# Retention attention and two feed-forward blocks on one core: two half units of a head pair in one TensorE visit, q by transposes, no filling matmuls in eight visits

## The chip, the cores and the metric

The kernel runs on one core of one Trainium2 chip. The metric is the device time of the core in microseconds, taken as the median of several executions. One further execution is recorded by the hardware profiler; all rows below come from that record of the kernel before.

## The reference

Three stages follow each other. The first is attention with a decay and without a softmax, the second a feed-forward block that takes the maximum of three projections, the third a gated feed-forward block.

```python
# attention: B, H, S, D = 4, 8, 576, 64
scores = scale * np.matmul(q, k.transpose(0, 1, 3, 2))
gamma = 1.0 - 2.0 ** (-5.0 - np.arange(H))
rel = pos[:, None] - pos[None, :]
Dmat = np.where(rel >= 0, gamma[:, None, None] ** rel, 0.0)
x = np.matmul(scores * Dmat, v)          # then (B*S, H*D) = (2304, 512)

# first block: w1, w2, w3 are (512, 768), w_out is (768, 512)
h = np.maximum(np.maximum(x @ w1, x @ w2), x @ w3)
x = h @ w_out

# second block: w_gate, w_val are (512, 1536), w_out2 is (1536, 512)
g = x @ w_gate
out = (g / (1 + np.exp(-g)) * (x @ w_val)) @ w_out2
```

## The kernel before

**Attention in units.** A unit is half of the 576 tokens (288, three chunks of 96) of one pair of heads of one batch; there are 32, in the order batch, head pair, half. Within a chunk the scores are computed directly; what earlier chunks contribute goes through a 64x64 state per head, which is carried from chunk to chunk with a decay. So a unit needs k and q with the head dimension on the partitions (kt and qg; qg is q times the decay g), k and v with the tokens on the partitions, and the states.

**What a unit does.** `a_prep(n)` makes ks (GpSimd), kt and qg. For the first PT = 12 units k and q come in rows of tokens and TensorE turns them: k by three transposes with the identity (L225), q by six matmuls against a diagonal matrix `dia` that holds the decay (L228); ScalarE copies both out of PSUM (L230). From unit 12 on k and q are loaded a second way by `t_load` (L188, eight loads of 32 columns, that is 128-byte pieces, for a pair of units, into a tile qk of which there are two); VectorE turns them in blocks of 32x32 and multiplies q by `cst_g`. `a_score(n)` is the group of six matmuls s (L248) and a multiplication by the decay mask on VectorE, giving pT. `a_state(n)` is the group m_ps (L264; four or six matmuls) and the chain of states on VectorE. `a_value(n)` is the group o_ps of states by q (L285; four or six) and of v by pT (L289; six). ScalarE then takes the upper part xh out of o_ps and VectorE the rest xl.

**Slices.** The first feed-forward block works on 288 tokens and 128 of the 768 columns at a time: one slice is twelve matmuls of 128x288 (L358) on the two-part splits of x and of the weights; ScalarE (w1) or VectorE (w2, w3: a maximum) takes it out of PSUM into hmax, and every third slice is stored. PSUM has two buffers for slices, one tile each for s, m_ps, o_ps and tp.

**Weights.** w1, w2 and w3 come as 18 tiles of 512 KB of double words, here w0 to w17 in the order of use (L106). Each is turned into two tiles by six steps: two passes on ScalarE (L115, L121), two instructions and a sum on VectorE (L123, L124, L126), wh on ScalarE (L134) and wlo on GpSimd (L136). A tile is loaded when the third step before it in the same buffers has been reached (`win_load(i + 4)`). After them come the weights of the second block (`early_steps`), some steps in each visit from unit 16 on.

**Order.** The order of all engines is the order of the program text. `visit(n)` does the value matmuls of unit n, the loads that are due, the states and scores of unit n + 1, and then a number of slices with `a_prep(n + 2)` and the conversion steps between them. Units 0 to 7 have no slices: their visits are the attention alone, and after each stands one filling matmul on zeros (`spin`, L380). Visits 8 to 13 have four slices, 14 and 15 six, later ones five. SyncE issues nearly all loads and stores, in program order, and a load into a buffer that is still read holds back those behind it. `a_load` of a pair is done in the odd visits, `t_load` in the even ones, for the pair two further on; `cst_g` is loaded in visit 9.

## Time and profile before

| | |
|---|---|
| median of three executions | 833.75 us (833.35 to 836.33) |
| the profiled execution | 833.75 us, span 831.6 us |
| TensorE busy | 817.6 us, 98% of the span |
| VectorE, ScalarE, GpSimd busy | 68%, 38%, 25% of the span |
| time in L358 (the slices' matmuls), three lines of 576 | 173.1 + 169.7 + 169.6 us |
| granted clock of TensorE | 1.00 in all stages |

The attention with its slices takes the first third of the span: the value matmuls of unit 11 begin at 67.92 us and those of the last unit at 273.3 us. Matmuls are pipelined, so the durations of neighbouring ones overlap and what one costs is read from start to start. In the timeline an f32 matmul of the attention counts twice, so "x12" is six matmuls. The DMA share is the mean over 16 engines, and a value near 1 says that they had work all the time.

### The profile page before, as it was taken

What the parts mean: (1) busy time and instruction counts of PE and PEld (TensorE: products, weight loads), DVE (VectorE), ACT (ScalarE), POOL (GpSimd) and SP (SyncE); (2) the same over time, 40 slices, a digit from 0 to 9 for tenths busy, and PEclk for the clock granted to TensorE, in tenths of its full rate; (3) what the DMA queues carried; (4) which work ended last, traced back from release to release, by engine and by line L of the source; (5) the groups of instructions that cost most, each with busy time, mean ns of one, the idle gap of its engine ahead of it and who ended that gap; (6) DMA issues with size and microseconds to landing.
All of it is one profiled execution on the core that took longest, in us unless ns stands there. A gap on an engine that the chain in (4) does not pass through costs nothing.

```text
span 831.6 us, 15514 instructions
## 1 busy us (share of the span) xinstructions
PE 817.6 (98%) x5933; PEld 762.7 (92%) x5933; DVE 563.4 (68%) x1007; ACT 315.0 (38%) x633; POOL 208.7 (25%) x194
## 2 busy tenths in 40 slices
PE   9999999999999999999999999999999999999998
PEld 6799899998989999999988999999998999999996
DVE  2678857787874354476587888888899455555554
ACT  3554523333321233565445553444443222332220
POOL 4243320000000002342023333233332333222331
PEclk9999999999999999999999999999999999999999
DMA  9999849999981223865555444334420716565522
GB/s 177 230 202 235 174 119 243 254 251 239 253 225 61 81 99 99 247 180 157 198 207 191 146 159 165 143 137 165 161 80 13 266 49 243 216 226 213 204 92 76
DMA packets 165801, 142.94 MB, mean 172 GB/s; under 512 B 101344, under 2 KB 137952, under 8 KB 165728
## 3 DMA queue, kind: packets, MB, share of 16 engines
q1 hardware_dynamic: 164368, 141.56, 57.7%
q8 instruction: 46, 0.75, 0.4%
q10 hardware_dynamic: 1360, 0.41, 0.2%
q14 instruction: 27, 0.22, 0.1%
HBM read 93.70 MB, written 48.23 MB: 171 GB/s over the span
## 4 chain that ended last, share of the span: by engine, by line
PE 68%; issue 14%; DVE 7%; POOL 6%; ACT 2%; DMA 1%; SPq 1%; POOLq 0%; ACTq 0%; DVEq 0%
PE ps L358 26%; PE g L786 17%; PE ps L763 11%; PE ps L715 6%; POOL gl L834 3%; PE s L248 2%; PE o_ps L289 2%; POOL p L807 2%; PE o_ps L285 2%; PE m_ps L264 1%; SPq L188 1%; PE tp L228 1%; PE psz L380 1%; DMA w<-in_moe_w_val_dram 1%; DVE wz L124 0%
## 5 line engine op out<-in xcount | busy, mean ns | idle before, releaser
L358 PE MATMUL ps<-xl,wh 128*128 128x288 f32 x576 | 173.1, 300 | 3.7 <-DVE hmax L364 3.1
L358 PE MATMUL ps<-xh,wh 128*128 128x288 f32 x576 | 169.7, 295 | 0.0
L358 PE MATMUL ps<-xh,wlo 128*128 128x288 f32 x576 | 169.6, 294 | 0.0
L834 POOL TENSOR_TENSOR gl<-p,gh 128x384 fp32r<-128x384 f32 x72 | 85.8, 1209 | 293.7 <-ACT gh L833 293.7
L763 PE MATMUL ps<-wp,gh 128*128 128x512 f32 (+1 forms) x436 | 135.3, 391 | 0.4 <-DVE acc L768 0.3
L358 PEld LDWEIGHTS ps<-xl,wh 128*128 128x128 f32 x576 | 108.0, 188 | 7.6 <-DVE hmax L364 4.0
L358 PEld LDWEIGHTS ps<-xh,wh 128*128 128x128 f32 x576 | 108.1, 188 | 0.0
L358 PEld LDWEIGHTS ps<-xh,wlo 128*128 128x128 f32 x576 | 108.1, 188 | 0.0
L763 PEld LDWEIGHTS ps<-wp,gh 128*128 128x128 f32 x436 | 80.7, 188 | 14.4 <-DVE acc L768 1.0
L364 DVE TENSOR_TENSOR hmax<-ps,hmax 128x288 f32<-128x288 f32 x96 | 43.6, 455 | 68.6 <-PE ps L358 61.9
L763 PE MATMUL ps<-wp,gl 128*128 128x512 f32 (+1 forms) x218 | 85.6, 393 | 0.0
L768 DVE TENSOR_TENSOR acc<-ps,acc 128x512 f32<-128x512 f32 (+1 forms) x91 | 62.2, 684 | 33.6 <-PE ps L763 31.6
L786 PE MATMUL g<-xhB,wa 128*128 128x384 f32 x288 | 73.4, 336 | 0.0
L786 PE MATMUL g<-xhT,wc 128*128 128x384 f32 x288 | 73.2, 335 | 0.0
L546 POOL TENSOR_TENSOR hl<-hf,hh 128x384 fp32r<-128x384 f32 x26 | 30.0, 1163 | 129.3 <-DMA h_d<-hmax 77.4
L833 ACT ACTIVATE gh<-p 128x384 fp32r<-128x384 f32 x72 | 37.8, 525 | 60.4 <-DVE p L837 53.2
L822 ACT ACTIVATE sb<-u 128x384 f32<-128x384 f32 x36 | 18.9, 525 | 110.0 <-DVE u L820 110.0
L218 POOL TENSOR_TENSOR ks<-kn,cst_a 96x384 f32<-96x384 f32 (+1 forms) x32 | 26.3, 825 | 126.1 <-PE m_ps L264 107.6
L786 PEld LDWEIGHTS g<-xhB,wa 128*128 128x128 f32 x288 | 52.1, 188 | 0.0
L786 PEld LDWEIGHTS g<-xhT,wc 128*128 128x128 f32 x288 | 52.0, 188 | 0.0
L814 DVE TENSOR_TENSOR p<-g,p 128x384 f32<-128x384 f32 x36 | 19.9, 554 | 46.4 <-PE g L786 40.6
L362 ACT ACTIVATE hmax<-ps 128x288 f32<-128x288 f32 x48 | 19.7, 410 | 81.4 <-PE ps L358 81.2
(119 smaller groups left out, 1710.9 us busy)
## 6 DMA issues: line engine op xcount, KB each, us to landing
w<-in_moe_w_out_dram SPq DMA_DIRECT2D x18, 512.0 KB, 4.1
w<-l_d SPq DMA_DIRECT2D x28, 256.0 KB, 2.9
h_d<-hmax SPq DMA_DIRECT2D x48, 144.0 KB, 3.3
w<-in_moe_w_dram SPq DMA_DIRECT2D x12, 512.0 KB, 5.9
w<-in_moe_w_gate_dram SPq DMA_DIRECT2D x12, 512.0 KB, 5.8
w<-in_moe_w_val_dram SPq DMA_DIRECT2D x12, 512.0 KB, 6.0
vn<-in_v_dram SPq DMA_DIRECT2D x16, 288.0 KB, 7.6
out_dram<-acc SPq DMA_DIRECT2D x17, 256.0 KB, 2.0
```

The source lines that it names most:

```text
L218: pool.tensor_tensor(u["ks"][:, 0:nk], u["k"][:, 0:nk], sc, ALU.mult)
L358: pe.matmul(ps, l[:, ksl], r, start=n == 0, stop=n == 3 * KD - 1)
L362: act.activation(mx[hb], ps, ACTF.Copy)
L364: dve.tensor_tensor(mx[hb], ps, mx[hb], ALU.max)
L546: (dve if fi in (3, 5) and hx else pool).tensor_tensor(hl, hf, f(hh), ALU.subtract)
L715: pe.matmul(ps[:, 0:HT], l[:, es], rr, start=n == 0, stop=n == 3 * F1 - 1)
L763: pe.matmul(ps[:, cs], l[:, sl], r[:, cs], start=n == 0, stop=n == 3 * GRP - 1)
L768: dve.tensor_tensor(a[:, cs], ps[:, cs], a[:, cs], ALU.add)
L786: pe.matmul(ps, l[:, ks], r[:, kc], start=first and n == 0, stop=n == 5, skip_group_check=True)
L814: dve.tensor_tensor(p5, g2, p5, ALU.add)
L833: act.activation(gh[half], t, ACTF.Copy)
L834: pool.tensor_tensor(gl[half], t, f(gh[half]), ALU.subtract)
```

## The change

- **Pairs.** From unit 12 on the two halves of a head pair are one visit (`visit_pair`, ten of them, for pairs 6 to 15): one group of ten and one of twelve matmuls for the values (`pair_value`), one group of ten for the states and one of twelve for the scores of the next pair (`pair_next`), then as many slices as the two visits had: eight, twelve, and ten from pair 8 on. States and chain follow in `late` steps between the slices. PSUM is given out anew in visit 11 (`swap_banks`, after xl of unit 11): four banks for scores and states, two for values.
- **q by transposes.** Units 0 to 11 transpose q as they do k. The tables `dia` go; ScalarE copies kt alone and VectorE multiplies q by `cst_g` on its way out of PSUM. `cst_g` is loaded at the start on ScalarE's queue, behind its loads of q.
- **Filling matmuls.** The eight behind visits 0 to 7 go. Those ahead of the first visit stay.
- **Loads.** `t_load` is done in each of visits 8 to 11 (pairs 6 to 9) and in each pair visit (for the pair three further on). So the qk tile of pair 9 is loaded in visit 11 and again in the visit of pair 6. `kq` has four buffers, not three.
- **Conversions.** In the visits of pairs 6 and 7 the plan has five and four tiles, spread over the first eight slices; from pair 8 on there are 17 early steps a pair, where two visits had 18.

```diff
+    def swap_banks():
+        nonlocal psa_cm, psa
+        psa_cm.__exit__(None, None, None)
+        psa_cm = tc.tile_pool(name="ps_pair", bufs=1, space=PSUM)
+        psa = psa_cm.__enter__()
...
-        kq = att.tile([P, 2, C], F32, name="kq", tag="kq", bufs=3)
+        kq = att.tile([P, 2, C], F32, name="kq", tag="kq", bufs=4)
...
             tp = psa.tile([P, 2, 512], F32, name="tp", tag="tp")
-            for c in range(NC):
-                pe.transpose(tp[:, 0, c * CK:(c + 1) * CK], u["k"][:, c].rearrange("p h d -> p (h d)"), ident)
-            for c in range(NC):
-                for e in range(2):
-                    pe.matmul(tp[64 * e:64 * e + 64, 1, c * CK:(c + 1) * CK], u["q"][:, c, e],
-                              dia[pr][:, e], start=True, stop=True)
-            act.activation(kq, tp[:, :, 0:C], ACTF.Copy)
+            for i, nm in enumerate("kq"):
+                for c in range(NC):
+                    pe.transpose(tp[:, i, c * CK:(c + 1) * CK], u[nm][:, c].rearrange("p h d -> p (h d)"), ident)
+            act.activation(kt, tp[:, 0, 0:C], ACTF.Copy)
+            dve.tensor_tensor(qg, tp[:, 1, 0:C].rearrange("p (c m) -> p c m", c=NC), g, ALU.mult)
...
+    def pair_value(j):
+        o = psa.tile([P, 2, 512], F32, name="o_ps", tag="o2")
...
+        for xh, xl, h in low:
+            dve.tensor_tensor(xl, o[:, h, 0:C], f(xh), ALU.subtract)
+
+    def pair_next(j):
...
+        s = psa.tile([P, 4, 512], F32, name="s", tag="s4")
+        m = [s[:, h, C + c * D:C + (c + 1) * D] for h in range(2) for c in range(NC - h)]
...
+        return [chain_states, lambda: weigh(0), lambda: weigh(1)]
...
         if n % 2:
             a_load(n // 2 + 3)
-        else:
-            t_load(n // 2 + 2)
+        if n >= PT - 4:
+            t_load(n - 2)
...
-        a_state(n + 1)
+        if n + 1 < PT:
+            a_state(n + 1)
         low()
-        a_score(n + 1)
+        if n + 1 < PT:
+            a_score(n + 1)
+            late = []
+        else:
+            swap_banks()
+            late = pair_next(PT // 2)
+        ahead = [n + 2] if n < PT - 2 else [PT, PT + 1] if n < PT - 1 else [PT + 2, PT + 3]
...
+    def visit_pair(j, slices, convs):
+
+        share = sharing(min(slices, 8 if convs else slices), convs, j >= 8)
+        pair_value(j)
+        share(0)
+        a_load(j + 3)
+        t_load(j + 3)
...
+        late = pair_next(j + 1)
+        for x in range(slices + 1):
+            if late:
+                late.pop(0)()
+            if x in (3, 5):
+                a_prep(2 * j + 4 + (x == 5))
+            if x:
+                share(x)
+            if x < slices:
                 f_some(1)
...
     a_load(0, "q", 2, act)
+    act.dma_start(out=cst_g, in_=consts[:, O_G:NCONST])
     a_load(0, "v")
...
-    for n in range(NU):
+    for n in range(PT):
...
-        if n == 9:
-            sp.dma_start(out=cst_g, in_=consts[:, O_G:NCONST])
-        visit(n, *((0, 0) if n < 5 else (0, 1) if n < 8 else (4, 2) if n < 13 else (4, 3) if n < 14 else (6, 2) if n < 16 else (5, 0)))
-        if n < 8:
-            spin(1)
-        if n == 15:
+        visit(n, *((0, 0) if n < 5 else (0, 1) if n < 8 else (4, 2)))
+    for j in range(PT // 2, NU // 2):
+        visit_pair(j, *((8, 5) if j == 6 else (12, 4) if j == 7 else (10, 0)))
+        if j == 7:
             ask(1)
```

The order on the engines changes at three places. The first is TensorE around the visits of units 1 and 2, which have no slices: `tp` are the transposes of the unit two further on, `psz` the filling matmul. Before:

```order
L225 MATMUL tp<-cst_a,kn 128x96 x3
L228 MATMUL tp<-dia_83,qn 64x96 x6
L380 LDWEIGHTS zero
L380 MATMUL psz<-zero 128x512
L285 MATMUL o_ps<-kq,st 64x96 x6
L289 MATMUL o_ps<-pT,vn 64x96 x6
L264 MATMUL m_ps<-vn,ks 64x64 x6
L248 MATMUL s<-kq 96x96 x6
```

And after:

```order
L228 MATMUL tp<-cst_a,kn 128x96 x3
L228 MATMUL tp<-cst_a,qn 128x96 x3
L285 MATMUL o_ps<-kq,st 64x96 x6
L289 MATMUL o_ps<-pT,vn 64x96 x6
L264 MATMUL m_ps<-vn,ks 64x64 x6
L248 MATMUL s<-kq 96x96 x6
```

The value matmuls of a unit now stand right behind the transposes of the unit after the next, with three transposes of q where six matmuls stood.

The second place is TensorE at the start of a pair. Before, the second unit of the pair has its own four groups, with slices (L358) ahead and behind:

```order
L358 MATMUL ps<-xh,wh 128x288
L285 MATMUL o_ps<-kq,st 64x96 x6
L289 MATMUL o_ps<-pT,vn 64x96 x6
L264 MATMUL m_ps<-vn,ks 64x64 x6
L248 MATMUL s<-kq 96x96 x6
L358 MATMUL ps<-xl,wh 128x288
```

After, one visit has the groups of both units (and the slices are at L417):

```order
L417 MATMUL ps<-xh,wh 128x288
L304 MATMUL o_ps<-kq,st 64x96 x10
L309 MATMUL o_ps<-pT,vn 64x96 x12
L332 MATMUL s<-vn,ks 64x64 x10
L339 MATMUL s<-kq 96x96 x12
L417 MATMUL ps<-xl,wh 128x288
```

Four groups instead of eight, the states now in the tile of the scores, and one change from and to the slices instead of two.

The third place is SyncE's queue from visit 8 on, behind the qk set of pair 6. `w64e` and `w_` are weight tiles, `kn` and `vn` a pair's rows of k and v, `qk` its eight transposed loads, `h_d` stores of hmax. Before, the first two rows are w7 and w8, the third weight tile w9, the next w10 and w11:

```order
L106 DMA w_774<-in_moe_w_dram 128x4x128
L106 DMA w64e<-in_moe_w_dram 128x4x128
L504 DMA cst_g<-in_consts_dram 128x384
L167 DMA kn<-in_k_dram 96x12x64
L167 DMA vn<-in_v_dram 96x12x64
L106 DMA w64e<-in_moe_w_dram 128x4x128
L345 DMA h_d_57<-hmax 128x288
L345 DMA h_d_58<-hmax 128x288
L106 DMA w_986<-in_moe_w_dram 128x4x128
L188 DMA qk<-in_k_dram 32x18x32 x4
L188 DMA qk<-in_q_dram 32x18x32 x4
L106 DMA w_1053<-in_moe_w_dram 128x4x128
```

And after, from w8 on:

```order
L108 DMA w64e<-in_moe_w_dram 128x4x128
L169 DMA kn<-in_k_dram 96x12x64
L169 DMA vn<-in_v_dram 96x12x64
L190 DMA qk<-in_k_dram 32x18x32 x4
L190 DMA qk<-in_q_dram 32x18x32 x4
L108 DMA w64e<-in_moe_w_dram 128x4x128
L404 DMA h_d_57<-hmax 128x288
L404 DMA h_d_58<-hmax 128x288
L108 DMA w_947<-in_moe_w_dram 128x4x128
L190 DMA qk<-in_k_dram 32x18x32 x4
L190 DMA qk<-in_q_dram 32x18x32 x4
L108 DMA w_1014<-in_moe_w_dram 128x4x128
```

The set of pair 7 has moved ahead of w9, that of pair 8 stands ahead of w11, and `cst_g` has gone from the queue. Further on the set of pair 9 comes twice, ahead of w13 and ahead of w15:

```order
L190 DMA qk<-in_k_dram 32x18x32 x4
L190 DMA qk<-in_q_dram 32x18x32 x4
L404 DMA h_d_58<-hmax 128x288
L108 DMA w64e<-in_moe_w_dram 128x4x128 x2
L169 DMA kn<-in_k_dram 96x12x64
L169 DMA vn<-in_v_dram 96x12x64
L190 DMA qk<-in_k_dram 32x18x32 x4
L190 DMA qk<-in_q_dram 32x18x32 x4
L108 DMA w_1352<-in_moe_w_dram 128x4x128
```

## Rows read from the trace of the kernel before

**Rows 1.** Table by stretches: us, PE, PEld, DVE, ACT, POOL busy, PEclk, DMA share, GB/s.

```profile
0.00:40.00 40.00, 37.61 (x553) 27.52 (x553) 17.79 (x41) 17.28 (x35) 14.32 (x25) 1.00 1.13 199
40.00:100.00 60.00, 59.95 (x643) 56.28 (x640) 47.08 (x99) 31.57 (x63) 24.09 (x20) 1.00 0.96 213
...
120.00:240.00 120.00, 118.43 (x1203) 112.55 (x1202) 90.83 (x193) 43.44 (x89) 10.32 (x12) 1.00 0.97 249
```

**Rows 2.** Timeline of ScalarE (start, us, engine, line, operation, idle before): w4, w15.

```profile
44.09 0.68 ACT L115 ACTIVATE wz<-w64e 128x512 f32<-128x512 f32 x1 [1.14 <-DMA w64e<-in_moe_w_dram]
44.67 0.40 ACT L362 ACTIVATE hmax<-ps 128x288 f32<-128x288 f32 x1
...
91.21 0.66 ACT L115 ACTIVATE wz<-w 128x512 f32<-128x512 f32 x1
```

**Rows 3.** Tile views of w9, w10, pair 7's last q, w15: issue (first, last), landing.

```profile
L106 SPq DMA_DIRECT2D w64e<-in_moe_w_dram x1: 2948/2948/2948, 56.8 to 56.8; - x1
DMA to landing us min/median/max: 7.3/7.3/7.3
...
L106 SPq DMA_DIRECT2D w<-in_moe_w_dram x1: 423/423/423, 61.0 to 61.0; - x1
DMA to landing us min/median/max: 5.7/5.7/5.7
...
L188 SPq DMA_DIRECT2D qk<-in_q_dram x2: 498/917/1336, 67.0 to 68.4; - x2
DMA to landing us min/median/max: 2.8/2.9/3.0
...
L106 SPq DMA_DIRECT2D w<-in_moe_w_dram x1: 433/433/433, 84.5 to 84.5; - x1
DMA to landing us min/median/max: 4.4/4.4/4.4
```

**Rows 4.** Waits of TensorE from 20 to 118 us: total, times, longest.

```profile
PE ps L358 <- DVE hmax L364: 1.2, 1, 1.2
```

**Rows 5.** Timeline of TensorE, visits of units 1 and 2.

```profile
13.24 0.71 PE L285 MATMUL o_ps<-kq,st 64*64 64x96 f32 x12
13.88 0.72 PE L289 MATMUL o_ps<-pT,vn 96*64 96x96 f32 x12
14.43 0.52 PE L264 MATMUL m_ps<-vn,ks 96*64 96x64 f32 x12
14.88 0.75 PE L248 MATMUL s<-kq 64*96 64x96 f32 x12
15.56 0.47 PE L225 MATMUL tp<-cst_a,kn 96*128 96x96 f32 x3
15.96 0.72 PE L228 MATMUL tp<-dia,qn 96*64 96x96 f32 x12
16.61 0.39 PE L380 MATMUL psz<-zero 128*128 128x512 bf16 x1
16.93 0.55 PE L285 MATMUL o_ps<-kq,st 64*64 64x96 f32 x8
17.40 0.72 PE L289 MATMUL o_ps<-pT,vn 96*64 96x96 f32 x12
17.95 0.40 PE L264 MATMUL m_ps<-vn,ks 96*64 96x64 f32 x8
18.28 0.75 PE L248 MATMUL s<-kq 64*96 64x96 f32 x12
```

**Rows 6.** Timeline of TensorE: third slice of unit 8; value matmuls of unit 11.

```profile
45.99 0.40 PE L358 MATMUL ps<-xl,wh 128*128 128x288 f32 x1
46.23 0.30 PE L358 MATMUL ps<-xh,wlo 128*128 128x288 f32 x1
46.36 0.29 PE L358 MATMUL ps<-xh,wh 128*128 128x288 f32 x1
...
67.92 0.47 PE L285 MATMUL o_ps<-kq,st 64*64 64x96 f32 x6
```

More of the change, by code (lines that the diff above doesn't have):

```diff
@@ L42 @@
 O_E = O_KS + NP * 2
-O_Q = O_E + NP
-O_S = O_Q + H
+O_S = O_E + NP
 O_M = O_S + H
@@ L96, in retention_moe @@
     g_t = cst_g.rearrange("p (r m) -> p r m", r=NP)
-    dia = [att.tile([CK, 2, CK], F32, name=f"dia{i}", tag=f"dia{i}", bufs=1) for i in range(NP)]
     d_t = [att.tile([CK, 2, CK], F32, name=f"dm{i}", tag=f"dm{i}", bufs=1) for i in range(NP)]
@@ L294, in a_value @@
         return lambda: dve.tensor_tensor(xl, o, f(xh), ALU.subtract)
+    def pair_value(j):
+        o = psa.tile([P, 2, 512], F32, name="o_ps", tag="o2")
+        us = [U.pop(2 * j + h) for h in range(2)]
+        for h, u in enumerate(us):
+            for c in range(1 - h, NC):
+                for e in range(2):
+                    hd = slice(64 * e, 64 * e + 64)
+                    pe.matmul(o[hd, h, c * CK:(c + 1) * CK], u["st"][hd, h * NC + c], u["qg"][hd, c],
+                              start=c == 1 - h, stop=False, skip_group_check=True)
+        for h, u in enumerate(us):
+            for c in range(NC):
+                for e in range(2):
+                    pe.matmul(o[64 * e:64 * e + 64, h, c * CK:(c + 1) * CK], u["v"][:, c, e], u["pT"][:, e, c],
+                              start=False, stop=True, skip_group_check=True)
+        b, _, pr = units[2 * j]
+        low = []
+        for h in range(2):
+            xh, xl = [ffn.tile([P, C], F32R, name=f"x{x}", tag=f"x{x}{pr}", bufs=4) for x in "hl"]
+            act.activation(xh, o[:, h, 0:C], ACTF.Copy)
+            xs[(2 * b + h, pr)] = (xh, xl)
+            low.append((xh, xl, h))
+        for xh, xl, h in low:
+            dve.tensor_tensor(xl, o[:, h, 0:C], f(xh), ALU.subtract)
@@ L380, in spin, with sharing @@
             pe.matmul(ps, zero[:, 0:P], zero, start=True, stop=True)
-    def visit(n, slices, convs):
+    def sharing(spread, convs, joins):
         plan = list(conv_plan(convs))
@@ L387, in share @@
             nonlocal done
-            upto = len(plan) * (j + 1) // (slices + 1)
+            upto = len(plan) * (j + 1) // (spread + 1)
             for step in plan[done:upto]:
@@ L392, in share, with visit @@
             done = upto
-            if n >= 16:
+            if joins:
                 for _ in range(1 if j % 2 else 2):
                     next(early, None)
+        return share
+    def visit(n, slices, convs):
+        share = sharing(slices, convs, False)
         low = a_value(n)
@@ L414, in visit @@
             if j < slices:
+                f_some(1)
+    def visit_pair(j, slices, convs):
[4 more added lines that the diff above has]
+        t_load(j + 3)
+        if j % NP == NP - 1:
+            fq.extend((2 * (j // NP) + h, *w) for w in win_units for h in range(2))
+        late = pair_next(j + 1)
+        for x in range(slices + 1):
+            if late:
+                late.pop(0)()
+            if x in (3, 5):
[3 more added lines that the diff above has]
+            if x < slices:
                 f_some(1)
@@ L475, in retention_moe @@
     a_load(0, "q", 2, act)
+    act.dma_start(out=cst_g, in_=consts[:, O_G:NCONST])
     a_load(0, "v")
     def tables(pr):
-        for t, sc, src in ((dia, q_t, ident), (d_t, s_t, mask)):
-            pool.tensor_tensor(t[pr], src.unsqueeze(1).to_broadcast([CK, 2, CK]),
-                               sc[:, 2 * pr:2 * pr + 2].unsqueeze(2).to_broadcast([CK, 2, CK]), ALU.mult)
+        pool.tensor_tensor(d_t[pr], mask.unsqueeze(1).to_broadcast([CK, 2, CK]),
+                           s_t[:, 2 * pr:2 * pr + 2].unsqueeze(2).to_broadcast([CK, 2, CK]), ALU.mult)
     tables(0)
```

34 lines of the change are left out of this document (30 added, 4 removed).

## The prediction

> **What bounds the kernel now.** I read the table by stages first [rows 1]. TensorE is busy in 59.95 of the 60 us from 40 to 100 and in 118.43 of the 120 from 120 to 240, at a granted clock of 1.00, so what leaves TensorE could leave the total. The same rows say that a second resource is full: the DMA share is 1.13 up to 40 us, 0.96 up to 100, 0.97 from 120 to 240. So I then read the loads, each by its time to landing, against the instruction that needs it. They land in the order of their issue. ScalarE has waited 1.14 us for weight tile w4 when it starts its first pass at 44.09 [rows 2], and the loads behind it take 4.4 to 7.3 us from issue to landing [rows 3]: w9 lands at 56.8 + 7.3 = 64.1, w15 at 84.5 + 4.4 = 88.9, 2.3 ahead of its first pass at 91.21 [rows 2, 3]. The trace of before therefore balances TensorE against a full stream of loads whose lead over ScalarE is some 0 to 2 us. TensorE's own waits are small: 1.2 us for hmax between 20 and 118 [rows 4].
>
> **The change part by part.** *Filling matmuls and q.* One filling matmul takes 0.32 us from its start to the next (16.61 to 16.93); eight are 2.6 us. The q matmuls of a unit take 0.65 (15.96 to 16.61) [rows 5]; three more transposes cost 0.40 if they are as those of k (15.56 to 15.96) [rows 5], less if the two groups run on without a step between; I take 0.35, so 0.30 a unit and 3.6 us for twelve. TensorE's work before the slices of unit 8 (ten units' transposes and eight filling matmuls) falls by some 5.6 us.
>
> *The multiply by g goes to VectorE.* Twelve instructions over 288 columns of PSUM; the nearest row is ScalarE's hmax of that shape, 0.40 [rows 2]. VectorE has 22 us free of the first 40 [rows 1], so they hide, but the first needs cst_g, now issued behind ScalarE's four loads of q. Nothing in the trace has a load of this size so early; the shortest landing here is 2.8 us after the issue and the longest 7.3 [rows 3]. The first score is later by zero (if it lands with q) to some 5 us; for 192 KB behind q I take 1.9, nearer the small loads.
>
> *What the first stage nets.* Its loads are the same as before, in the same order, plus cst_g. Their landing is set by the stream, so w4 can land no earlier than 44.1; with cst_g ahead of it I take 44.9 (192 KB at the 199 to 249 GB/s of [rows 1] is 0.8 to 1.0; bounds 0 and 1.5). Behind w4 in ScalarE's order stands the hmax that empties the first slice of unit 8, and TensorE's third slice needs that buffer: w4 at 44.9, its pass and the hmax, 0.68 and 0.40 (0.58 and 0.3 to the next start), give 45.9 [rows 2]. Before, that slice starts at 45.99 [rows 6]. So the 5.6 us turn into TensorE waiting for w4, and this stage nets 0.0; only one unit's transposes come later, for -0.3. Bounds: 0 and -5.
>
> The Trainium skill (DMA: Bandwidth & Descriptors, Issuing engines are not separate DMA queues) says that loads started by ScalarE run on the same 16 engines and interleave with SyncE's. By that rule cst_g delays w4; if ScalarE's queue were a path of its own, w4 would stay at 44.1 and the total would be 0.8 lower. No run here shows it for cst_g.
>
> *Pairs.* A visit's four groups follow each other without a gap, so I split each step into a part per matmul and a part per group. The o_ps<-kq,st group takes 0.64 with 6 matmuls and 0.47 with 4: 0.085 each and 0.13 fixed. m_ps: 0.45 and 0.33, 0.06 each and 0.09 fixed. o_ps<-pT and s move 96 columns too: six at 0.085 to 0.09 leave 0.04 of the 0.55 and 0.14 of the 0.68 [rows 5]. A slice's first matmul behind other work takes 0.24 to the next, later ones 0.13 [rows 6]: 0.11 for leaving a visit, and for entering it I estimate 0.09. One visit for two saves the sum once, 0.60 us; ten pairs, -6.0. Bounds -4 (if the longer groups run no closer) and -7.
>
> *The order of loads.* The transposed k and q of a pair are eight loads of 128-byte pieces. The last one of pair 7 is issued at 68.4 and lands 2.8 later, at 71.2, w10 just ahead of the set at 61.0 + 5.7 = 66.7: a set takes 4.5 us of the stream [rows 3]. The new order puts the set of pair 7 ahead of w9, pair 8 ahead of w11, pair 9 ahead of w13, and pair 9 a second time ahead of w15 (visit 11 asks for it and so does pair visit 6). All 24 loads of the last three sets pass ahead of tiles that ScalarE needs within one visit, and each set waits for a free buffer, with SyncE's later loads queued behind it.
> - w9 lands at 64.1 + 4.5 = 68.6. On ScalarE the xh of unit 11 stands behind its two passes and the previous tile's wh: 68.6 + 3 x 0.58 + 0.4 = 70.7 [rows 2], and xl on VectorE some 0.5 later, 71.2. In visit 11 the PSUM pool changes hands after xl, so the state matmuls of pair 6 wait for it. In before unit 11's visit begins at 67.92 [rows 6]; with its value matmuls of about 1.1 TensorE reaches them at 69.0: +2.2 (bounds 0.7, the bare chain xh and xl, and 4.5).
> - w13 has two more sets ahead of it, 9 us. It sits in mid-visit, where two PSUM buffers cover two slices of 1.6 us; I take +0.3, bounds 0 and 4.
> - w15 lands at 88.9 and is used at 91.21 in before. Pair 9 twice, and its k and v (576 KB at the 213 GB/s of [rows 1], 2.7), push it by 11.7 to 100.6. Its use comes later too, by the terms above and as conversions stand some slices further back in the new plan; I estimate 95. ScalarE's hmax and VectorE's of the last slice wait behind it: 5.6 late, less two slices of 1.6 and an estimated 1.3 for the conversion steps that need no longer be waited for: +1.1, bounds 0 and 5. The six hmax, eight conversions and two preparations queued on VectorE behind it in pair visit 7 come in a burst; I estimate +1.5, bounds 0 and 3.
> - The 1.2 us of before [rows 4] lie in this stretch and are part of this: -1.2.
>
> *From pair visit 8 on* the early weight conversions run at 17 steps a pair, not 18, and the pair is 3% shorter, so the stream is as full as before (0.97). k, v and both transposes of a pair now come in one bunch, 4.5 + 2.7 us, ahead of the next weight tile: +0.5, bounds 0 and 5. VectorE's and GpSimd's other work is unchanged, and a pT has ten slices to be ready in.
>
> Sum: -0.3 - 6.0 + 2.2 + 0.3 + 1.1 + 1.5 - 1.2 + 0.5 = -1.9. The profiled execution took 833.75 us, span 831.6 and 2.15 around it, which is the median of the three: 831.85, say **832.0**.
>
> **The rivals.** *The lead covers the late tiles.* Conversions run some units ahead of the slices that use them, so late tiles might cost TensorE nothing but the bare handover: -0.3 - 6.0 + 0.7 - 1.2 = -6.8, **827.0**. For it: TensorE waits so little in before. Against it: the hmax that frees PSUM stands in the same queue as the late tile.
>
> *The loads come earlier too.* If the stream speeds up with TensorE, -5.6 + 1.9 is kept as well: 827.0 - 3.7, **823.3**. Against it: a share of 1.13.
>
> *The stream sets the end* (slower). If the loads pace everything from w4 to the last early tile at 250 us, TensorE's saved work becomes waiting, and what counts is the stream's own length: one set more, 4.5 us, **838.3**. It decides from the point at which w17 lands so late that the idle stretch after 100 us is used up. For it: shares of 0.96 and 0.97 [rows 1]. Against it: that stretch, which lies between the two full ones.
>
> *The clock.* TensorE will idle 2 us or so at the start, before the third slice of unit 8 and at the handover, with fewer filling matmuls. All rows here have a clock of 1.00, none shows the lower level, so I bound a fall by 0 and 2 us a place: up to 6, some **836**. The Trainium skill (TensorE: Matmul & The Clock Gate, Why this matters for your kernels) says that idle gaps put the clock back to 1.2 GHz. By that rule the sum would be up to 6 us higher, about 838; the trace has no gap long enough to test it.
>
> **How the numbers follow.** Forecast 0.50, lead covers 0.24, loads earlier 0.09, stream sets the end 0.13, clock 0.04. This measurement can tell about 0.5%, 4.2 us, from no change: the bounds are 829.6 and 837.9. The forecast's own bounds reach a little over both (0.03 below, 0.02 above). Faster: 0.24 + 0.09 + 0.03 = 0.36. Slower: 0.13 less the part that stays under 837.9 (0.04), with 0.02 and 0.01 of the clock, 0.12. Same 0.52. The range leaves out most of the fourth and of the second rival's far ends: 825.5 to 838.3.
>
> **What would show it.** Right: TensorE's third slice of unit 8 starts within 0.5 us of 45.99; w4, w9 and w15 land at about 44.9, 68.6 and 100.6; TensorE waits 2 us for xl at the first state matmuls of a pair, and more for hmax in pair visits 6 and 7 than before; pairs from the eighth on follow each other 0.6 us sooner than two visits and their ten slices did. Wrong: TensorE is 3 us or more ahead at that slice; the set of a pair lands in 2 us; the first pair visits run without waits.

## The result and the profile after

The changed kernel takes 846.71 us in the median of six executions (838.28 to 853.49), the kernel before 834.52 us beside it (832.79 to 836.33); the ratio is 1.0111, with an interval of 1.0078 to 1.0144. The ratios here and below leave out executions more than 1.5% above the fastest of their kernel, here the two longest, 850.86 and 853.49 us. So the change makes the kernel slower, by 1.1% (1.5% by the medians of all executions), and unsteady. The profiled execution is the shortest, 838.28 us with a span of 836.5; its mean granted clock is 0.988, and the longer the execution the lower the clock: 0.980 with 843.74, 0.972 with 848.37, 0.962 with 853.49. In the kernel before it is 1.00 throughout [rows 1].

The table by stretches of the changed kernel, first the stretches of [rows 1], then pairs of stretches around the places where the clock falls (us, PE, PEld, DVE, ACT, POOL busy, PEclk, DMA share, GB/s):

```profile
0.00:40.00 40.00, 32.60 (x447) 24.67 (x448) 21.05 (x50) 14.61 (x35) 12.00 (x21) 0.96 1.14 204
40.00:100.00 60.00, 55.41 (x560) 52.20 (x560) 46.55 (x93) 26.67 (x53) 22.11 (x20) 0.91 0.94 187
120.00:240.00 120.00, 119.21 (x1234) 115.37 (x1234) 86.58 (x186) 40.84 (x85) 10.29 (x13) 1.00 0.89 226
...
8.00:10.00 2.00, 0.91 (x19) 0.82 (x21) 0.50 (x2) 0.00 (x0) 0.00 (x0) 1.00 1.41 191
10.00:14.00 4.00, 4.00 (x47) 3.11 (x43) 1.66 (x4) 0.75 (x3) 2.32 (x4) 0.57 1.41 185
38.00:41.00 3.00, 0.97 (x19) 0.79 (x20) 2.05 (x6) 2.42 (x6) 1.84 (x2) 1.00 1.11 252
41.00:45.00 4.00, 4.00 (x38) 3.71 (x35) 3.76 (x9) 1.50 (x3) 1.46 (x2) 0.57 1.28 226
70.00:72.00 2.00, 0.07 (x2) 0.00 (x0) 1.97 (x5) 0.89 (x2) 0.18 (x1) 0.96 0.78 123
72.00:78.00 6.00, 5.37 (x52) 5.11 (x53) 1.98 (x7) 0.94 (x3) 2.06 (x2) 0.50 0.85 209
100.00:102.00 2.00, 0.52 (x4) 0.52 (x5) 1.86 (x5) 0.63 (x1) 0.20 (x1) 1.00 0.80 100
102.00:109.00 7.00, 5.98 (x35) 5.35 (x35) 5.58 (x11) 3.12 (x5) 2.52 (x2) 0.54 1.02 323
```

Each of the four times the order is the same: TensorE stands idle for a late input (waits of 2.0, 2.0, 2.6 and 2.2 us, the last with a second one of 1.0), then it works again, and about then its clock goes to the lower level (0.50 of 2.4 GHz, that is 1.2) for 3 to 6 us. A stretch of 4 us at 0.57 costs 1.7 us of full speed; the four together cost 1.7 + 1.7 + 2.7 + 2.7, some 9 us (6 and 7 us at 0.50 and 0.54, of which only the busy part counts). An estimate from these rows: without them this execution would have ended at about 829.

TensorE's longest waits up to 300 us (total, times, longest). In the kernel before there were 1.2 us for hmax [rows 4], 0.8 for xl and 0.2 for ks between 20 and 118:

```profile
PE o_ps L285 <- DVE xl L294: 3.7, 3, 2.0
PE ps L417 <- DVE hmax L423: 3.4, 3, 2.2
PE s L332 <- issue: 2.6, 1, 2.6
PE s L248 <- DVE kq L230: 2.0, 1, 2.0
PE ps L417 <- ACT hmax L421: 1.7, 3, 0.8
```

How far behind the kernel before it is at the start of the value matmuls of a unit or pair:

| | before | after | difference |
|---|---|---|---|
| unit 0 | 9.84 | 11.78 | +1.9 |
| unit 5 | 27.41 | 27.16 | -0.3 |
| unit 8 | 39.59 | 40.03 | +0.4 |
| unit 11 | 67.92 | 68.71 | +0.8 |
| pair 6 (unit 12) | 76.80 | 83.79 | +7.0 |
| pair 7 | 94.26 | 108.06 | +13.8 |
| pair 8 | 119.82 | 132.14 | +12.3 |
| pair 15 | 267.91 | 274.14 | +6.2 |

All that is lost is lost ahead of pair 7; from pair 8 on the change gains, 6.1 us in seven pairs. From pair 6 on the rows show the lag some 1.1 us too large, since the changed kernel has the states and scores of both halves of the pair behind it there, and the kernel before those of one half: the next stage (w_out) begins at 337.06 us against 331.95, +5.1.

### The profile page after: what moved, and what is told of

It reads as the page before. It is cut to its first block, busy times and chain, and to the rows that moved or that the text cites. A ratio compares the mean times of both kernels' runs of the same rounds, so it can differ in the third digit from the quotient of the medians.

```text
span 836.5 us, 15290 instructions
## 1 busy us (share of the span) xinstructions
PE 813.3 (97%) x5817; PEld 763.9 (91%) x5817; DVE 569.9 (68%) x1019; ACT 312.3 (37%) x633; POOL 205.2 (25%) x190
## 4 chain that ended last, share of the span: by engine, by line
PE 68%; issue 14%; DVE 8%; POOL 6%; ACT 2%; DMA 2%; SPq 1%; ACTq 0%; POOLq 0%; DVEq 0%
PE ps L417 26%; PE g L878 16%; PE ps L855 11%; PE ps L807 7%; POOL gl L926 3%; POOL p L899 2%; PE s L339 1%; PE o_ps L309 1%; PE o_ps L304 1%; PE s L248 1%; PE o_ps L289 1%; PE s L332 1%; PE o_ps L285 1%; PE tp L228 1%; DVE wz L125 1%
## 5 line engine op out<-in xcount | busy, mean ns | idle before, releaser
L417 PE MATMUL ps<-xl,wh 128*128 128x288 f32 x576 | 174.2, 302 | 5.3 <-DVE hmax L423 3.4
L417 PE MATMUL ps<-xh,wh 128*128 128x288 f32 x576 | 171.3, 297 | 0.0
L417 PE MATMUL ps<-xh,wlo 128*128 128x288 f32 x576 | 171.2, 297 | 0.0
L417 PEld LDWEIGHTS ps<-xl,wh 128*128 128x128 f32 x576 | 109.6, 190 | 9.5 <-DVE hmax L423 5.6
L417 PEld LDWEIGHTS ps<-xh,wlo 128*128 128x128 f32 x576 | 109.7, 190 | 0.0
L417 PEld LDWEIGHTS ps<-xh,wh 128*128 128x128 f32 x576 | 109.6, 190 | 0.0
```

The costliest lines, as they stand in the source:

```text
L417: pe.matmul(ps, l[:, ksl], r, start=n == 0, stop=n == 3 * KD - 1)
```

## The experiments

Each run is compared with the kernel before on the same chip (833.3 to 834.1 us in all of them).

**The filling matmuls back.** The edit:

```diff
         visit(n, *((0, 0) if n < 5 else (0, 1) if n < 8 else (4, 2)))
+        if n < 8:
+            spin(1)
```

> The changed kernel with the eight filling matmuls back behind visits 0 to 7, all else as changed. Theory: TensorE's clock falls after it has idled for a late input (2.0 us for cst_g at 7 us, 2.0 us for xl at 38 us, 2.6 us at the change of PSUM pools at 70 us, 4.5 us in pair visit 6), and the filling matmuls only take 0.32 us out of the second of these: 836 to 839 us, clock 0.99, falls at 10, 72 and 103 us still there. Rival: the missing filling matmuls are what lets the clock fall: clock 1.00 in all stretches, about 829 to 832 us.

845.72 us (844.54 to 847.16), ratio 1.0143 (1.0127 to 1.0160), where I expected 836 to 839. No gain: the rival on the filling matmuls falls, but so does my size for the first fall. Here TensorE waits 3.0 us for cst_g and then runs at half clock from 10 to 31 us, not for 3.5 us.

**The qk sets in the old order.** The edit:

```diff
-        if n >= PT - 4:
-            t_load(n - 2)
+        if n >= PT - 4 and n != 9:
+            t_load({8: 6, 10: 7, 11: 8}[n])
```

> The changed kernel with the qk sets loaded in the order of before (pair 6 in visit 8, pair 7 in visit 10, pair 8 in visit 11, pair 9 once, in the visit of pair 6). Theory: the qk sets that were moved forward, with SyncE held for a free buffer and pair 9 loaded twice, are what makes w9, w13 and w15 late: w9 lands at about 64, w13 at about 81, the 2.6 us wait at the change of pools shrinks under 1, the 4.5 us of waits in pair visit 6 go, the falls of the clock at 72 and 103 us go with them: 825 to 828 us, clock about 0.996. Rival: the change of PSUM pools and the denser pair visits idle TensorE by themselves: waits and falls stay, 834 us or more.

840.09 us (839.04 to 840.61 and one of 853.64), ratio 1.0076 (1.0060 to 1.0093), which overlaps that of the changed kernel. The theory falls. Weight tile w9 lands at 54.8 + 8.2 = 63.0, a little ahead of the 64.1 of the kernel before:

```profile
L108 SPq DMA_DIRECT2D w64e<-in_moe_w_dram x1: 3742/3742/3742, 54.8 to 54.8; - x1
DMA to landing us min/median/max: 8.2/8.2/8.2
```

and yet TensorE waits as long at the change of pools (timeline of the same run):

```profile
73.28 0.38 PE L332 MATMUL s<-vn,ks 96*64 96x64 f32 x2 [2.58 <-issue]
```

In the changed kernel w9 lands 4.6 us later, at 63.3 + 4.3 = 67.6, and the wait is 2.56. The four waits in pair visit 6 are the same too, 0.78, 0.46, 2.19 and 1.08 us against 0.79, 0.46, 2.22 and 1.02. So it is not the loads alone. What both have is VectorE's queue. VectorE in the changed kernel at the change of pools and in pair visit 6 (start, us):

```profile
70.03 0.45 DVE L423 TENSOR_TENSOR hmax<-ps,hmax 128x288 f32<-128x288 f32 x1
70.39 0.68 DVE L128 CUSTOM_DVE_ANT_0 wl<-wz,wl 128x1024 uint16<-128x1024 uint16 x1
...
72.07 0.46 DVE L294 TENSOR_TENSOR xl<-o_ps,xh 128x288 fp32r<-128x288 f32 x1
...
92.98 1.36 DVE L125 TENSOR_SCALAR wz<-wz 128x512 uint32<-128x512 uint32 x1
...
97.18 1.57 DVE L235 TENSOR_TENSOR kq<-qt,cst_g 128x288 f32<-128x288 f32 x1
...
100.98 0.45 DVE L423 TENSOR_TENSOR hmax<-ps,hmax 128x288 f32<-128x288 f32 x1
```

ScalarE between them:

```profile
71.11 0.63 ACT L136 ACTIVATE wh<-wl 128x512 fp32r<-128x512 f32 x1 [2.25 <-DVE wl L128]
71.65 0.39 ACT L292 ACTIVATE xh<-o_ps 128x288 fp32r<-128x288 f32 x1
```

VectorE has had two preparations, a conversion and an hmax to do since 65.6 without a gap; its wl comes at 71.1, ScalarE's wh waits for that, xh stands behind wh, and xl behind xh, at 72.07. The state matmuls of pair 6 take over the banks that xl still reads, and start at 72.63. In pair visit 6 VectorE goes from one instruction to the next from 92 to 106.9 us, and the hmax that frees a slice's buffer comes at 100.98 behind a preparation and a conversion.

Part of that queue is VectorE's own instructions taking longer. The L235 at 97.18 takes 1.57 us and the L125 at 92.98 1.36, where they take 0.46 and 0.42 when GpSimd does nothing beside them; here GpSimd is at work at the same time:

```profile
68.59 0.46 DVE L235 TENSOR_TENSOR kq<-qt,cst_g 128x288 f32<-128x288 f32 x1
...
97.14 1.29 POOL L138 TENSOR_TENSOR wlo<-wl,wh 128x512 fp32r<-128x512 f32 x1 [2.12 <-ACT wh L136]
98.39 0.84 POOL L220 TENSOR_TENSOR ks<-kn,cst_a 96x256 f32<-96x256 f32 x1
```

Five such instructions between 92 and 104 us are 3.7 us longer together, against the 4.5 us that TensorE waits there. Not every instruction is stretched: hmax, which reads PSUM, takes 0.45 beside GpSimd as without it. What the waits would be without this no run shows.

**TensorE's idle places filled.** The edit:

```diff
-    spin(2)
+    spin(8)
     a_score(0)
...
         visit(n, *((0, 0) if n < 5 else (0, 1) if n < 8 else (4, 2)))
+        if n in (6, 7):
+            spin(2 * n - 8)
...
+            spin(8)
             swap_banks()
```

> The changed kernel with filling matmuls put into three of its four idle places: six more ahead of the first scores, four behind visit 6 and six behind visit 7, eight ahead of the change of pools in visit 11. Theory: the loads stay as late as they are, and the waits as long, but the clock holds at 1.00 up to 80 us; what comes back is the slow running alone, 1.6 + 1.6 + 3.2 us: about 832 us, with the fall at 103 us still there. Rival: the falls cost nothing since the loads pace this part: 837 to 839 us. Rival: filling does not hold the clock: clock as in the changed kernel.

838.24 us (835.67 to 843.84), ratio 1.0066 (1.0032 to 1.0100): less than the changed kernel takes, but not the 832 that I expected. In the profiled execution, the slowest of the five, the clock holds at 1.00 up to 70 us, although TensorE waits 1.6 us ahead of the first scores, and unit 11 starts at 67.30, 1.4 us ahead of the changed kernel. At the change of pools it still falls, since eight filling matmuls end before the wait, which is 3.9 us here. The w_out stage takes 79.4 us where the changed kernel takes 75.8 (first matmul to the first of the next stage); TensorE waits 1.3 us in it for hl, which VectorE makes from stored hmax. Why is not known.

**The first part of the change alone.** The edit, on the kernel before:

```diff
-                    pe.matmul(tp[64 * e:64 * e + 64, 1, c * CK:(c + 1) * CK], u["q"][:, c, e],
-                              dia[pr][:, e], start=True, stop=True)
-            act.activation(kq, tp[:, :, 0:C], ACTF.Copy)
+                    pe.transpose(tp[:, i, c * CK:(c + 1) * CK], u[nm][:, c].rearrange("p h d -> p (h d)"), ident)
+            act.activation(kt, tp[:, 0, 0:C], ACTF.Copy)
+            dve.tensor_tensor(qg, tp[:, 1, 0:C].rearrange("p (c m) -> p c m", c=NC), g, ALU.mult)
...
+    act.dma_start(out=cst_g, in_=consts[:, O_G:NCONST])
...
-        if n < 8:
-            spin(1)
```

> The kernel before with the first part of the change alone: q of the first twelve units by transposes with the multiply by cst_g on VectorE, cst_g loaded at the start, no filling matmuls behind visits 0 to 7; no pairs, and the qk loads as before. Theory: as in the changed kernel the first scores start 1.8 us later, the clock falls at 10 us, and visits 7 and 8 wait for xl, so the value matmuls of unit 8 start 0.4 us later than before and the clock falls once more behind that: +1 to +2, 834.5 to 836 us. Rival: the work taken off TensorE comes through: 829 to 831 us. Rival: this part holds most of the loss: 838 us or more.

846.96 us (840.76 to 851.92), ratio 1.0159 (1.0107 to 1.0212): as much as the whole change costs. The rival that this part holds most of the loss is right. The table by stretches of its profiled execution (848.14 us):

```profile
8.00:10.00 2.00, 0.10 (x2) 0.10 (x2) 0.46 (x1) 0.00 (x0) 0.00 (x0) 0.97 1.41 183
10.00:36.00 26.00, 26.00 (x259) 21.98 (x259) 10.34 (x24) 4.56 (x13) 5.23 (x8) 0.50 1.05 191
```

TensorE waits 3.2 us for cst_g ahead of the first scores and then works without a gap at half speed for 26 us. But not every wait is followed by that: in the third stage of this execution TensorE waits 2.31 us (up to 450.97), and the clock stays at 1.00.

**The first columns of cst_g early**, in the first part alone and in the changed kernel:

```diff
     act.dma_start(out=cst_a, in_=consts[:, 0:O_G])
+    act.dma_start(out=cst_g[:, 0:CK], in_=consts[:, O_G:O_G + CK])
...
-    act.dma_start(out=cst_g, in_=consts[:, O_G:NCONST])
+    act.dma_start(out=cst_g[:, CK:], in_=consts[:, O_G + CK:NCONST])
```

> The kernel before with the first part of the change alone, as in the run of that part, but the 96 columns of cst_g that the first head pair needs (48 KB) are loaded on ScalarE's queue ahead of q, the rest behind it as before. Theory: the long slow stretch at the start (half clock from 10 to 37 us in that run, from 10 to 13.5 in the profile of the changed kernel) is set off by the 2 to 3 us in which TensorE waits for cst_g; without the wait the clock stays at 1.00 up to 40 us and the total is 832 to 836 us with little spread. Rival: the first stage without filling matmuls is too thin for the clock in any case: half clock remains, 840 us or more.

843.34 us (836.03 to 852.49), ratio 1.0083 (1.0056 to 1.0110).

> The changed kernel with the first 96 columns of cst_g ahead of q, nothing else. Theory: no fall of the clock at the start, the other three places (xl at 38 us, the change of pools at 70 us, pair visit 6) as in the changed kernel: 836 to 838 us, and the spread of 838 to 853 us between executions gone. Rival: the spread comes from the later places: a spread of 10 us or more stays.

846.87 us (846.30 to 848.96), ratio 1.0157 (1.0129 to 1.0185).

Both miss. The wait for cst_g is shorter but not gone: in the first run TensorE still stands idle 0.6 us for q and 1.2 us for kq around the first scores, and then (table by stretches, the profiled execution of 852.49 us):

```profile
10.00:56.00 46.00, 46.00 (x450) 39.04 (x449) 24.57 (x57) 14.78 (x34) 10.01 (x13) 0.50 0.99 187
```

It is busy in all of 46 us, at half speed. Gaps of 0.6 and 1.2 us came before it. They need not lead to it: the second run of the mended pairs below, which has the same start, waits 0.5 and 1.1 us at the same places in its profiled execution, and its first 36 us are at 1.00 and at the durations of full speed. In the second of the two runs here, the wait of 2.2 us in pair visit 6, behind which the clock falls in the changed kernel, is there as well, and the matmuls behind it follow each other at full speed (0.13 us from start to start; timeline):

```profile
112.37 0.40 PE L417 MATMUL ps<-xl,wh 128*128 128x288 f32 x1 [2.19 <-DVE hmax L423]
112.60 0.29 PE L417 MATMUL ps<-xh,wlo 128*128 128x288 f32 x1
112.73 0.29 PE L417 MATMUL ps<-xh,wh 128*128 128x288 f32 x1
```

**The pairs mended, with that start.** Two slices ahead of the change of pools; then also the old order of the qk sets and another plan of conversions:

```diff
+            f_some(2)
             swap_banks()
...
-        visit_pair(j, *((8, 5) if j == 6 else (12, 4) if j == 7 else (10, 0)))
+        visit_pair(j, *((8, 3) if j == 6 else (12, 6) if j == 7 else (10, 0)))
```

> As the run with cst_g early, and two of the four slices of visit 11 are put between its value matmuls and the change of PSUM pools, so that TensorE has 3.2 us of work while VectorE comes to xl. Theory: VectorE's queue (two preparations, a conversion, hmax) sets the end of xl there, not the landing of w9, since the wait was the same 2.6 us with w9 4.6 us earlier; TensorE then waits under 0.5 us and the fall at 72 us goes: 5 us less than with cst_g early alone, 831 to 833 us. Rival: the slices make their own wait for hmax and only move the idle time: within 1.5 us of cst_g early alone.

840.38 us (833.96 to 846.71), ratio 1.0061 (1.0035 to 1.0086).

> As the run before it, with the qk sets loaded in the order of the kernel before and once each, and the conversions of pair visits 6 and 7 planned as three and six tiles where they were five and four. Theory: in pair visit 6 VectorE has no gap from 94 to 106 us; with two conversions less (some 1.8 us of VectorE each) the hmax come in time, the 4.5 us of waits and the fall at 103 us go: 824 to 828 us, clock above 0.997. Rival: the conversions only move, and the waits come in pair visit 7: 830 us or more.

843.85 us (833.63 to 847.74), ratio 1.0110 (1.0067 to 1.0152). Both miss, and the medians say little, since the start is as unsteady as before. The profiled executions (837.27 and 833.63 us) say more. The wait at the change of pools is gone in both (0.6 us for ks are left). In the first, the rival is right in part: a wait of 2.4 us for hmax, with a fall of the clock, comes up at 89 us, where the changed kernel has none; two later ones of 2.2 and 1.6 us have no fall behind them. In the second, the four waits in the middle of pair visit 6 and their fall are gone, that new one is still there, and the w_out stage begins at 328.7 us, 3.2 ahead of the kernel before and 8.3 ahead of the changed kernel. Since moving the loads alone changed no wait, this points to the conversions; no run changes them alone.

**The start in the kernel before, and the start filled.** Three runs that ask for the cause of the unsteady start: the changed kernel with spin(8) for spin(2) ahead of the first scores; the kernel before without the eight filling matmuls of its visits; and the kernel before with a gap at the start:

```diff
     a_prep(0)
-    spin(2)
     a_score(0)
     a_state(0)
     a_prep(1)
-    spin(1)
```

> The changed kernel with eight filling matmuls ahead of the first scores where it has two, nothing else. Theory: what lets the first stage run at half clock, for 3.5 us in one execution and up to 50 in others, is the idle stretch of 2 to 3 us ahead of the first scores, not the number of filling matmuls later; with it shortened the first 38 us run at 1.00 and the total is 835 to 840 us, without executions above 842. Rival: the visits are too thin in any case: executions of 845 us and more remain.

840.30 us (837.92 to 848.92), ratio 1.0099 (1.0061 to 1.0136). A miss in the spread: in the profiled execution (846.74 us) cst_g landed at 10.2 us, not 8.5, and 3.5 us of the wait were left.

> The kernel before without the eight filling matmuls behind visits 0 to 7, nothing else: the start, the diagonal tables and all loads as before. Theory: the start keeps TensorE busy and the clock at 1.00, TensorE gains 2.6 us by unit 7 and waits for xl instead, as weight tiles set the pace there: within 1 us of before, one fall at 40 us at most (+1.6). Rival: these eight are what holds the clock: half clock in the first 40 us, +5 us or more.

832.97 us (831.11 to 835.62), ratio 0.9988 (0.9978 to 0.9999). As expected: unit 7 starts 1.1 us earlier, behind a wait for xl of 0.7 us, and the clock holds:

```profile
0.00:40.00 40.00, 36.09 (x567) 27.70 (x567) 18.94 (x43) 17.59 (x35) 14.30 (x25) 1.00 1.16 196
```

> The kernel before without the two filling matmuls ahead of the first scores and the one ahead of the first visit, nothing else. Theory: a gap at the start is enough to leave the first stage at half clock for a time that differs from execution to execution, in a kernel that has nothing of the change: +3 to +15 us with a spread of several us. Rival: without the change's wait for cst_g nothing happens: within 1 us of before, clock 1.00.

838.60 us (832.52 to 855.91), ratio 1.0025 (0.9998 to 1.0052). Four of the ten executions are like those of the kernel before (832.5 to 834.6), and three are at 845.93, 848.06 and 855.91, where 22 of the kernel before on the same chip took at most 837.88. So the kernel before, with three filling matmuls fewer at its start, is as unsteady as the changed one; the ratio alone, without these three, is not clear of no change. Its profiled execution (837.34 us) has waits of 0.7 and 0.5 us around the first scores, and then:

```profile
10.00:20.00 10.00, 10.00 (x108) 8.04 (x106) 2.05 (x6) 2.35 (x5) 4.62 (x8) 0.51 1.11 177
```

So the eight filling matmuls in the visits do nothing that can be measured, and without the three at the start the clock can fall.

**All filled, a miss.** With early cst_g, the filled start, filling matmuls behind visits 6 and 7, the mends of the pairs, and in all pairs the states and pT two slices later:

```diff
-            if late:
+            if late and x >= 2:
                 late.pop(0)()
```

> The changed kernel with everything that the runs so far point to: the first columns of cst_g early, eight filling matmuls ahead of the first scores, four and six behind visits 6 and 7, two slices of visit 11 ahead of the change of pools, qk sets in the old order and once each, conversions planned as three and six, and the states and pT of a pair put two slices later so that hmax comes first on VectorE. Theory: no idle stretch over 1.5 us up to 130 us and the clock at 1.00; the pairs' gain of some 6 us is left: 824 to 829 us, a spread under 4 us. Rival: VectorE's work in the visits of pairs 6 and 7 idles TensorE anyhow: 831 us or more.

842.98 us (841.45 to 844.50), ratio 1.0108 (1.0088 to 1.0129). The clock is 1.00 in every stretch and the spread 3 us, as expected; but the states and pT now stand on VectorE where they hold up hmax in every pair (waits of TensorE up to 300 us):

```profile
PE ps L417 <- DVE hmax L423: 11.0, 13, 1.4
```

The time is far from the 824 to 829 that I expected. Here the w_out stage is 4 us longer as well (79.8 us), as in the first filled run.

**The start mended, then the pairs, then the rest.** The first run is the changed kernel with early cst_g and spin(8) together.

> The changed kernel with both mends of its start together: the first 96 columns of cst_g ahead of q, and eight filling matmuls ahead of the first scores; each alone had left a gap (1.2 us and 3.5 us). Theory: TensorE enters visit 0 without an idle stretch, all executions run the first 38 us at 1.00, and the spread that the changed kernel has between executions goes; left are xl at 38 us, the change of pools and pair visit 6 with their three falls: 835 to 838 us, all executions within 3 us. Rival: the spread comes from these three: executions at 843 us or more remain.

841.12 us (838.50 to 843.37), ratio 1.0087 (1.0056 to 1.0118). In the profiled execution the first 38 us are at 1.00, and no execution is above 843.4; but the median is 3 us above what I expected, 5 us of spread stay, and the other falls are there (table by stretches, 838.50 us):

```profile
0.00:38.00 38.00, 31.81 (x455) 23.91 (x455) 21.17 (x50) 14.65 (x35) 11.93 (x21) 1.00 1.11 201
38.00:44.00 6.00, 5.98 (x58) 5.50 (x59) 5.70 (x12) 2.62 (x6) 2.86 (x3) 0.72 1.20 252
68.00:78.00 10.00, 7.44 (x67) 7.15 (x66) 5.95 (x15) 3.84 (x8) 2.23 (x2) 0.66 1.05 224
100.00:108.00 8.00, 7.01 (x52) 6.27 (x52) 5.85 (x11) 3.79 (x6) 2.40 (x3) 0.57 0.96 287
```

> The same start, and the three mends of the pairs (two slices of visit 11 ahead of the change of pools, qk sets in the old order and once each, conversions planned as three and six), without moving the states and pT back. Theory: as in the run that had these mends with an unsteady start, whose profiled execution ended the first stage 3.3 us earlier than the kernel before, but now in every execution: 826 to 830 us. Rival: the third stage gives it back through the waits for a store that two filled runs showed: 831 us or more.

833.81 us (832.32 to 838.78), ratio 0.9996 (0.9976 to 1.0016). The three mends of the pairs are worth 7 us; the w_out stage begins at 328.9. The total is some 4 us above what I expected: falls at 38, 88 and 436 us remain, behind waits of 2.0, 2.4 and 2.5 us. The last of these, in the third stage, is for p from ScalarE:

```profile
435.04 0.69 PE L880 MATMUL g<-xlB,wa 128*128 128x384 f32 x1 [2.48 <-ACT p L890]
```

In the kernel before and in the changed kernel this wait is 0.6 us. Here the third stage takes 2.6 us longer than in the kernel before (404.76 to 812.49 us against 408.00 to 813.14), nearly all of the 3.0 us that the profiled execution was ahead. So the rival was right that the third stage gives it back, though not by a wait for a store. The same wait of 2.1 us or more stands in eight of the fifteen runs; what sets it off is not known.

The last has filling matmuls behind visits 6 and 7 as well, and in the visit of pair 6 alone the states and pT one slice later.

> As the run before it, with four and six filling matmuls behind visits 6 and 7 against the fall at 38 us, and the states of the next pair one slice later in the visit of pair 6 alone, so that hmax does not wait for them. Theory: the falls at 38 and 88 us (1.5 to 2 us each) go too, and the 11 us of waits for hmax that came from moving states and pT in all pairs do not come back: 823 to 828 us with a clock above 0.998. Rival: as the run before it within 1 us.

832.00 us (829.34 to 834.52), ratio 0.9978 (0.9961 to 0.9995): the first version of the change that is faster than the kernel before, by 0.2%, and 1.3% under the changed kernel by the two ratios. The kernel before without its eight filling matmuls comes to 0.9988 (0.9978 to 0.9999), which overlaps it, and I had expected 4 us less. Its table by stretches:

```profile
0.00:40.00 40.00, 35.75 (x463) 25.24 (x463) 20.92 (x50) 14.40 (x35) 11.83 (x21) 1.00 1.09 195
40.00:100.00 60.00, 56.86 (x622) 53.16 (x624) 48.83 (x102) 27.37 (x54) 23.07 (x21) 1.00 0.98 200
120.00:240.00 120.00, 119.40 (x1238) 115.72 (x1236) 89.44 (x194) 42.01 (x87) 9.33 (x12) 1.00 0.90 235
```

The clock is 1.00 in all three; TensorE still waits 3.8 us for hmax and 2.3 for xl up to 300 us, and 1.8 us in the w_out stage. Up to that stage the profiled execution gains only 0.5 us on the run before it (328.42 against 328.93 us). The w_out stage is then 2 us longer, and the third stage 2.6 us shorter, without the long wait for p.

## Why the prediction was wrong

**The step that failed is the clock.** It had no term in my sum. I put it last among the rivals, with a chance of 0.04 and 0 to 2 us a place, because no row of the kernel before shows the lower level. Measured are four places in the shortest execution, some 9 us; and the first of them, 3.5 us long there, is up to 46 us long in other runs with a wait at the same place. Two of the idle stretches that it stands behind were in my own working: 1.9 us for cst_g at the start, which I let vanish in a wait for w4, and 2.2 us for xl at the change of pools. I booked each at its own length or less and did not ask what TensorE does behind it. The rule of the Trainium skill that I named (TensorE: Matmul & The Clock Gate, Why this matters for your kernels), that idle gaps put the clock back to 1.2 GHz, agrees with these runs in one direction: every fall shown here stands behind a wait, and in the two runs with all places filled or mended its mean is 1.000 and 0.999. It does not hold the other way: waits of 2.2 to 2.3 us in three other runs were followed by no fall. And the waits of 2.0 to 2.6 us that were followed by one are shorter than the gaps that the page warns of; here the measurement decides. The sum by that rule, 838, is what the shortest execution gave (838.28), by luck: it stood for three places of up to 2 us on top of 832, and what was measured is some 9 us in four places on top of about 829, in the fastest of six executions. That the price differs between executions, 838 to 853 us, I had not thought of at all.

Point by point, in the profiled execution:

- *q by transposes.* Right: three take 0.34 us (26.82 to 27.16), I took 0.35.
- *The wait for cst_g.* Right in size: the first scores start at 9.09, 1.8 us later than before. The rows of TensorE:

```profile
9.09 0.75 PE L248 MATMUL s<-kq 64*96 64x96 f32 x12 [2.01 <-DVE kq L230]
...
11.78 0.91 PE L285 MATMUL o_ps<-kq,st 64*64 64x96 f32 x8
```

  It is x8 in 0.91 us here and 0.55 before [rows 5]: the clock. The edit that I costed at nothing beyond its wait is the dearest of the change: the first part alone costs 13.6 us in the median.
- *The filling matmuls.* Half right. In the visits they were worth nothing either way (ratio 0.9988); I had not looked at those of the start, which stay in the change but do not cover the longer wait.
- *The first stage nets nothing.* Right in size up to unit 8 (+0.4 us), by another way: w4 lands at 42.0, 2 us earlier than before and not at 44.9, and TensorE waits 1.5 and 2.0 us for xl, which stands behind wh on ScalarE. So the landing of w4 was not set by the stream as I had it. The third slice of unit 8 starts at 47.4 us, where I said 45.9: the scores ahead of the slices and half of the first slice ran at half speed.
- *The change of pools.* Right in size (2.56 us, I took 2.2), half wrong in its cause: w9 did land at 67.6 (I said 68.6) and ScalarE did wait for it, but VectorE's queue came to the same time, and sets it when w9 is early, as the run with the old order of loads shows.
- *Late w13 and w15.* w15 landed at 104.7 (I said 100.6), and the waits in pair visit 6 are 4.5 us where my three terms had 2.9 for both visits. Again VectorE and not the loads: with the loads early the waits are the same, and with two conversions fewer there they go (that run also has the loads early).
- *Pairs.* Right: pair 8 takes 19.96 us where its two visits took 20.64, -0.68 against my -0.60:

```profile
132.14 1.04 PE L304 MATMUL o_ps<-kq,st 64*64 64x96 f32 x20
152.10 1.04 PE L304 MATMUL o_ps<-kq,st 64*64 64x96 f32 x20
```

  Seven of them are 4.8 us; with the waits of 0.5, 1.0 and 0.9 us for hmax of before that went, less 0.7 of new ones, that makes 6.5, near the 6.1 us gained from pair 8 to 15. The +0.5 for loads in bunches did not show.
- *The rivals.* "The stream sets the end" gave a time on the right side, 838.3, by a mechanism that the runs speak against: with the old order of loads and one set fewer, no wait at the change of pools or in pair visit 6 moved, and in the changed kernel itself the DMA share from 120 to 240 us is 0.89, not 0.97. The clock rival had the mechanism, and too small a price.

What stays open: why a wait is followed by the lower level in one execution and not in another, why the slow start lasts 3.5 us in one run and 46 in another, why the w_out stage is 2 to 4 us longer in three of the filled runs (and 2.7 us in the first part with cst_g early, which has no filling), and why the wait for p in the third stage is 0.6 us in some executions and over 2 in others.

## What to carry to other kernels

Where a change lets TensorE stand idle for a microsecond or more, ask what speed it comes back at: in the shortest execution here the price of a wait of 2 us or more was its length and about as much again behind it; at the start, in other executions, it was many times that, and in some runs nothing. Filling matmuls are worth what stands behind them: the eight in the thin visits covered nothing and the three at the start kept the clock up there in the kernel before, so each group is tried by itself before it is removed. And when a late load looks like the cause of a wait, move the load alone; two chains ended together here (ScalarE's second pass over w9 at 68.86 us, VectorE's preparations at 68.97), and only the run with early loads told them apart.

## What the runs showed of the hardware

- After a gap at the start TensorE can be busy without a break for 46 us at 0.50, as in the run of the first part with cst_g early. There the clock rose at about 56 us, one microsecond into the slices of unit 8 (55.06). In the run of the first part without early cst_g it rose at 37 us, in the middle of the visits without slices.
- A granted clock of 1.00 in the table does not always go with the durations of full speed. In the profiled execution of the changed kernel with cst_g early, the stretch from 8 to 38 us is shown at 1.00:

```profile
8.00:38.00 30.00, 30.00 (x293) 25.25 (x295) 12.48 (x29) 6.13 (x16) 5.19 (x8) 1.00 1.17 205
```

  and yet its matmuls take the time of the lower level, 1.23 us where six of this kind take 0.71 at full speed [rows 5]:

```profile
16.34 1.23 PE L285 MATMUL o_ps<-kq,st 64*64 64x96 f32 x12
```

  The run of the mended pairs with slices first shows the same from 10 to 14 us. Whether the row or the clock is off there is not known; so the durations are read beside the clock.
- The same load landed at 8.1 to 9.3 us in four executions on one chip, and at 10.2 on another (cst_g behind q, issued at 4.1 to 4.4 us); the gap ahead of the first scores was 2.0 us in the changed kernel, where it landed at 8.5, and 3.5 us where it landed at 10.2.
- Some VectorE instructions take longer while GpSimd works and others do not. In the trace of the changed kernel from 20 to 270 us no L235 without GpSimd beside it took more than 0.46 us, and beside it they took up to 1.57; L125 took up to 0.43 and up to 1.36. hmax, xl, pT and the transposes took the same beside it (0.45, 0.45, 0.74, 0.47 and 0.43 us).
